# Turning the keys of the third block on with VectorE and GpSimd in place of TensorE, in a fused attention and feed-forward kernel

## Chip, cores and metric

The kernel runs on one core of one Trainium2 chip. The metric is the device time of one execution in microseconds (us); the time given is the median of three runs. The inputs and outputs are float32.

## What is computed

A gated linear recurrence over 768 steps gives the input of a two-layer feed-forward block with a squared ReLU:

```python
f = 1.0 / (1.0 + np.exp(-f_logit))
for t in range(S):
    state = f[:, :, t, :, None] * state + np.einsum('bhd,bhe->bhde', k[:, :, t], v[:, :, t])
    y[:, :, t] = np.einsum('bhd,bhde->bhe', q[:, :, t], state)
x = y.transpose(0, 2, 1, 3).reshape(B * S, H * D)     # 3072 x 384
h = x @ w_in                                          # 384 x 2048
r = np.maximum(h, 0.0)
out = (r * r) @ w_out                                 # 2048 x 384
```

with 4 batches, 8 heads, 768 steps and a head size of 48.

## The kernel before

The 768 steps are cut into six blocks of 128 steps (all four batches together, 512 columns). A **unit** is one block and one pair of heads: unit n has block n // 4 and pair n % 4. The first three units of a block are "own" units; the fourth has no rows of its own and works on rows that the other three have put aside in `last_kq` and `last_kn`. Units 0 to 7 (the first two blocks) run in a prologue whose order is written out by hand (FIRST, SECOND). What matters here starts after it.

From there the feed-forward runs as a row of **pieces** (`Moe.flow`): 16 pieces for the second block, 10 for the rest of the first, then 16 for each further block. A piece n is nine matmuls `up` (L244, tile `ph`), ScalarE's ReLU, square and cast (L254 to L256, tile `gh`), VectorE's remainder (L261, tile `gl`), and nine matmuls `down` of the piece two earlier (L271). Each product is made of three matmuls on halves of the float32 words. In the first 14 pieces VectorE and ScalarE also decode weights (L141 to L171).

Between pieces stand the **slots** of the attention: `SLOTS` says after which piece. The slot with unit n as the new one and n-1 as the old one issues on TensorE the updates of the state of unit n (L558, tile `shared`), its scores (L574) and the outputs of unit n-1 (L623, L632). The updates for the first 64 steps of each batch (c = 0) come first and those for the other 64 (c = 1) at the slot's end. All of them write one bank of PSUM. Between the two, GpSimd writes a flag (L768, `G.memset(tick, 0)`): it waits for the last c = 0 update, and the first c = 1 update waits for it.

What a unit needs before its slot is a list of stages, each with a piece relative to its slot (`STAGE_AT`, `BLOCKS_AT`):

- L and v: loads, on SyncE's queue
- G: the gate on ScalarE (L447)
- K: VectorE's scan of the keys (L452), GpSimd's two small clamps of 128x8 (L457, tiles `fkq` and `low`), VectorE's product (L458)
- Q: VectorE's reciprocal of the clamped column (L464), scan (L466) and product (L469)
- T: four TensorE transposes of the keys into PSUM (L514), for the units below `TURNED` = 13
- B: for the others, VectorE's transpose inside blocks of 32x32 (L528), then 16 copies of blocks on GpSimd (L533)
- N: for the units below 13 ScalarE's copy of the turned keys out of PSUM (L538, tile `kn`); for all of them ScalarE's copy of the put-aside columns (L540, `last_kn`)
- s: two copies of states on ScalarE (L487)

After a slot VectorE does the mask (L588) and the states (L603, L610) of the new unit, ScalarE and VectorE the cast and the remainder of the old unit's output (L652, L668).

Each engine works through its instructions in the order in which the compiled program has them. For VectorE, ScalarE, TensorE and SyncE this is the order of the code; GpSimd's comes from the same code, through the scheduler.

Of the kernel before, what the change touches and what calls it, by code (L numbers as in the profile page):

```python
# [13 lines left out]
F32 = mybir.dt.float32  # L14
F32R = mybir.dt.float32r
# [7 lines left out]
P = 128  # L23
B, H, S, D = 4, 8, 768, 48
DM, DFF = 384, 2048
HP = H // 2
C = 64
# [3 lines left out]
NT = B * TB  # L31
NZ = B * NC
# [9 lines left out]

LAG = 2
Q = 32
TURNED = 13
AHEAD = 4
LO = 6
SPLIT = 2
# [7 lines left out]

SLOTS = (13, 16, 19, 21, 23, 27, 31, 35, 39, 43, 47, 51, 55, 59, 63, 67, 71)
STAGE_AT = ((-6, 0, "Lv"), (-3, 1, "GK"), (-1, 0.5, "Q"), (-1, 1, "TN"), (1, 1, "s"))  # L60
BLOCKS_AT = ((-6, 0, "Lv"), (-3, 1, "GKB"), (-1, 0.5, "Q"), (0, 0.7, "N"), (1, 1, "s"))
LAST_AT = ((-6, 0, "v"), (1, 1, "s"))


# [295 lines left out]
    return t.rearrange("p (n t) -> p n t", t=C)  # L360


def scanned(t):
    return t.rearrange("p (n t) -> p n t", t=CZ)


def fast_path(ctx, psum, tc, moe, ident, low, flag, fkqT, vN, w, w4, out):
# [41 lines left out]
    class Unit:  # L409
# [93 lines left out]

        def turn(self):

            if self.blk < 2:
                self.pk = self.ps_a[0].tile([P, B, P], F32, tag="pk", name=f"pk{self.nm}")
            else:

                if not shared:  # L510
                    shared.append(self.ps_a[0].tile([P, B, P], F32, tag="pk", name="shared"))
                self.pk = shared[0]
            for b in range(B):
                nc.tensor.transpose(  # L514
                    out=self.pk[:, b], in_=self.kt[:, b * TB : (b + 1) * TB], identity=ident
                )

        def turn_blocks(self):


            if self.n < 14:
                both = self.wk([P, 2, NT], "ys")
                kb, kn = both[:, 0], both[:, 1]
            else:
                kb, kn = (
                    moe.gp.tile([P, NT], F32, tag=f"part{i}", name=f"turn{self.nm}_{i}", bufs=1) for i in range(2)
                )
            V.transpose(out=kb, in_=self.kt)  # L528
            kb, self.kn = (t.rearrange("p (b n) -> p b n", b=B) for t in (kb, kn))
            self.pk = self.kn  # L530
            for a in range(0, P, Q):
                for r in range(0, P, Q):
                    G.tensor_copy(out=self.kn[a : a + Q, :, r : r + Q], in_=kb[r : r + Q, :, a : a + Q])  # L533

        def turned(self):
            if self.n < TURNED:
                self.kn = self.wk([P, B, ROWS], "kn")
                nc.scalar.copy(out=self.kn, in_=self.pk[:, :, :ROWS])  # L538
            at = self.hp * (C - D)
            nc.scalar.copy(  # L540
                out=last_kn.rearrange("p b (h r) -> p b h r", h=2)[:, :, :, at : at + C - D],
                in_=self.pk.rearrange("p b (h r) -> p b h r", h=2)[:, :, :, D:],
            )
# [10 lines left out]

        def add_one(self, dd, b, c, h):

            rows, m = slice(c * C, (c + 1) * C), D if h or self.blk > 1 else C
            return nc.tensor.matmul(  # L558
                dd[h * C : h * C + m, c, b * D : (b + 1) * D],
                lhsT=self.kn[rows, b, h * C : h * C + m],  # L560
                rhs=self.vn[rows, b, h * D : (h + 1) * D], start=True, stop=True,
            )
# [81 lines left out]
        def upper(self):  # L644

            self.x = self.xs[self.blk]
            y = self.x[self.hp] if self.own else self.wk([ROWS, 2, NT], "ys", 1, F32R)
            if not self.own:
                self.x.append(y)
            self.y = [y[:ROWS, i].rearrange("p (b c t) -> p c b t", b=B, c=NC) for i in range(2)]  # L650
            self.py = self.py[:ROWS].rearrange("p c (b t) -> p c b t", t=C)
            nc.scalar.copy(out=self.y[0], in_=self.py)  # L652
# [26 lines left out]
        def stage(self, letters):  # L679
            for c in letters:  # L680
                {
                    "L": lambda: self.load(slice(0, 3)),
                    "f": lambda: self.load(slice(0, 1)),
                    "k": lambda: self.load(slice(1, 2), slice(2, 3)),
                    "v": lambda: self.load_v(),
                    "G": lambda: self.gates(),
                    "K": lambda: self.keys(),
                    "Q": lambda: self.queries(),
                    "m": lambda: self.move(),
                    "r": lambda: self.crossed(),  # L690
                    "T": lambda: self.turn(),
                    "B": lambda: self.turn_blocks(),
                    "N": lambda: self.turned(),
                    "D": lambda: self.add(),
                    "S": lambda: self.scores(),
                    "M": lambda: self.masked(),
                    "C": lambda: self.states(),
                    "s": lambda: self.crossed_states(),
                    "Y": lambda: self.outputs(),
                    "H": lambda: self.upper(),  # L700
                    "z": lambda: self.less(),
                    "X": lambda: self.lower(),
                    "g": lambda: self.parts((1,), G if self.blk < 2 else nc.sync),
                    "h": lambda: self.parts((0,), nc.sync),
                }[c]()
# [7 lines left out]
    )  # L713
    half = list(range(LO)), list(range(LO, NF))
    xs = {blk: moe.new_x(blk, blk) for blk in range(2)}
    units, decoding, shared = {}, {}, []

    for t in xs[0]:
        G.memset(t[C + 32 :].bitcast(F32), 0.0)
# [10 lines left out]
    def slot(old, new):  # L730

        ab = ps_a.tile([P, 2, 512], F32, tag="ab", name=f"ab{(new or old).nm}_{new is None}")
        rows = [[], []]
        if old:
            old.py = ab[:, :, : B * C]
            for c in range(NC):
                for b in range(B):  # L740
                    for part in range(2):
                        for h in (c, 1 - c):
                            rows[c].append((C, lambda a=(part, b, c, h): old.output_one(*a)))
        if new:
            new.sd = ab[:, :, B * C :]
            new.dd = shared[0].rearrange("p (c e) n -> p c (e n)", c=NC)[:, :, : B * D]
            adds = [
                [] if new.last_of(c) else [
                    (D, lambda a=(b, c, h): update(*a)) for b in range(B) for h in (c, 1 - c)
                ] for c in range(NC)  # L750
            ]
            for h in range(2):
                for b in range(B):
                    for c in (h, 1 - h):
                        rows[h].append((C, lambda a=(b, c, h): new.score_one(*a)))
            rows = [adds[0] + rows[0], rows[1] + adds[1]]
        seen = []

        def behind(ins, first):
            tc.add_manual_dep(ins, first.name, mybir.DependencyInfo(  # L760
                mybir.DependencyClass.Sync, mybir.DependencyReason.DATA
            ), reason="one bank")

        def update(b, c, h):
            ins = new.add_one(new.dd, b, c, h).ins
            if c == 0 and b == B - 1 and h:

                seen.append(G.memset(tick, 0).ins)  # L768
                behind(seen[0], ins)
            elif c and b == 0 and h:  # L770
                behind(ins, seen[0])

        at = [0, 0]
        while any(rows):
            r = min((r for r in range(2) if rows[r]), key=lambda r: at[r])
            cols, do = rows[r].pop(0)
            at[r] += cols
            do()
# [51 lines left out]
    with tc.manual_schedule(engines={ET.PE, ET.SP, ET.DVE, ET.Activation}):  # L830
# [13 lines left out]
        def hook(n, at, do):  # L844
            hooks.setdefault((max(n, 0), at), []).append(do)

        def third():
            early.close()
            moe.inputs(ctx)
            xs[2] = moe.new_x(2, 2)  # L850

# [2 lines left out]
        for n in range(1, NF - 1):  # L856
# [22 lines left out]
            hook(n, 0, before)  # L879
            hook(n, 0.5, after)  # L880
            hook(n, 0.7, last)
        hook(NF - 1, 0, third)
        late = [Unit(n, xs, (ps_a,)) for n in range(2 * HP, NBLK * HP)]
        for at, old, un in zip(SLOTS, (None, *late), (*late, None)):
            if un:
                for n, place, stage in LAST_AT if not un.own else STAGE_AT if un.n < TURNED else BLOCKS_AT:
                    hook(at + n, place, lambda un=un, stage=stage: un.stage(stage))
            hook(at, 1, lambda old=old, un=un: slot(old, un))
            if old:
                hook(at, 1, lambda old=old: old.stage("HX" if old.own else "HXhg"))  # L890
            if un:
                hook(at, 1, lambda un=un: un.stage("rMCm" if un.own else "rMC"))
# [238 lines left out]
```

## Time and profile before

| | |
|---|---|
| median of three runs | 485.92 us (485.27 to 486.57) |
| profiled execution, its own time | 483.37 us |
| span of the profiled execution | 481.7 us |
| TensorE matmuls busy | 468.2 us, 97% of the span |
| VectorE, ScalarE, GpSimd busy | 54%, 58%, 17% |
| granted TensorE clock, mean | 0.999 |

The profile is one execution, so durations are taken from it and a sum of them is set against its own time, 483.37 us. A group's row in the trace gives the busy time and the mean duration of one instruction, a row of the timeline its start and duration in us. The start-to-start distance of neighbours is what an instruction costs its engine; the recorded durations of matmuls overlap.

### The profile page before, as it was taken

To read this page: it belongs to the slowest core of one execution; us is meant where nothing else is said; L and a number is where in the kernel's file an instruction comes from. 1 tells how busy PE (TensorE), PEld (TensorE's weight loads), DVE (VectorE), ACT (ScalarE), POOL (GpSimd) and SP (SyncE) were. 2 spreads that over 40 slices of the span, in tenths; PEclk is the share of its full clock that TensorE was granted. 3 is DMA by queue.
4 is the path that set the end of the run, shared out by engine and by line. 5 is a ranking of instruction groups with operands and counts; after the bars stand their busy time and mean duration, and the time that the engine had idled before them with its cause. 6 is when DMAs were issued, how large, how long until landed. Compare 5 with 4: busy or idle time off the path is not lost. (4 is left out here: it accounts for less than half of the span.)

```text
span 481.7 us, 11552 instructions
## 1 busy us (share of the span) xinstructions
PE 468.2 (97%) x4763; PEld 384.9 (80%) x4763; DVE 261.5 (54%) x482; ACT 277.9 (58%) x562; POOL 80.0 (17%) x210
## 2 busy tenths in 40 slices
PE   5889999999999999999999999999999999999996
PEld 5767787888888888888888888888888888888884
DVE  7999976988966566643447443356353312221111
ACT  4778757787756555645546645545654543544441
POOL 6222010001010005150053150052350000000000
PEclk9999999999999999999999999999999999999999
DMA  8995235567114205332005332005300002100002
GB/s 292 282 310 141 66 95 182 191 221 254 28 31 141 86 2 125 95 97 80 1 2 127 95 95 83 1 1 122 98 12 3 2 0 34 67 0 2 1 0 71
DMA packets 22636, 42.60 MB, mean 88 GB/s; under 512 B 4512, under 2 KB 8128, under 8 KB 22576
## 3 DMA queue, kind: packets, MB, share of 16 engines
q1 hardware_dynamic: 22128, 40.86, 27.6%
q0 software_dynamic: 448, 0.92, 0.8%
q8 instruction: 39, 0.64, 0.6%
q14 instruction: 21, 0.17, 0.1%
HBM read 31.69 MB, written 4.72 MB: 76 GB/s over the span
## 5 line engine op out<-in xcount | busy, mean ns | idle before, releaser
L244 PE MATMUL ph<-x,w 128*128 128x512 f32 x864 | 215.1, 393 | 1.1 <-DVE gl L261 0.6
L244 PEld LDWEIGHTS ph<-x,w 128*128 128x128 f32 x864 | 160.0, 188 | 35.6 <-DVE gl L261 1.0
L271 PE MATMUL po<-gh,w 128*128 128x512 f32 x570 | 175.5, 389 | 0.0
L261 DVE TENSOR_TENSOR gl<-ph,gh 128x512 fp32r<-128x512 f32 x95 | 65.4, 688 | 160.0 <-ACT gh L256 159.7
L254 ACT ACTIVATE ph<-ph 128x512 f32<-128x512 f32 x96 | 55.9, 582 | 123.9 <-PE ph L244 123.7
L271 PEld LDWEIGHTS po<-gh,w 128*128 128x128 f32 x570 | 107.0, 188 | 22.3
L271 PE MATMUL po<-gl,w 128*128 128x512 f32 x285 | 111.1, 390 | 0.0
L271 PEld LDWEIGHTS po<-gl,w 128*128 128x128 f32 x285 | 53.5, 188 | 11.2
L255 ACT ACTIVATE ph<-ph 128x512 f32<-128x512 f32 x96 | 55.9, 582 | 3.0
L256 ACT CAST gh<-ph 128x512 fp32r<-128x512 f32 x95 | 55.8, 587 | 3.0
L533 POOL COPY turn<-turn 32x128 f32<-32x128 f32 x112 | 42.1, 376 | 8.3 <-DVE turn L528 3.7
L457 POOL TENSOR_SCALAR fkq<-fkq 128x8 f32<-128x8 f32 x18 | 12.9, 717 | 144.9 <-DVE fkq L452 128.2
L452 DVE TENSOR_TENSOR_SCAN fkq<-fz,dr 128x520 f32<-128x520 f32 x18 | 22.3, 1238 | 6.7 <-ACT fz L447 6.7
L169 ACT CAST w<-wa 128x384 fp32r<-128x384 f32 (+1 forms) x33 | 16.6, 513 | 14.8 <-DVE wa L156 11.7
L466 DVE TENSOR_TENSOR_SCAN fkq<-fz,dz 128x520 f32<-128x520 f32 x18 | 22.4, 1247 | 0.6
L623 PE MATMUL ab_False<-sc,vn 64*48 64x64 f32 (+1 forms) x480 | 20.7, 220 | 0.0
L141 ACT ACTIVATE wa<-raw 128x384 f32<-128x384 f32 (+1 forms) x33 | 18.1, 550 | 4.1 <-DMA raw<-in_w_dram 4.1
L668 DVE TENSOR_TENSOR x<-ab_False,x 112x512 fp32r<-112x512 f32 x12 | 8.3, 692 | 21.7 <-ACT x L652 21.7
L652 ACT CAST x<-ab_False 112x512 fp32r<-112x512 f32 x12 | 7.0, 587 | 22.5 <-PE shared L558 17.6
L632 PE MATMUL ab_False<-rx,sx 48*48 48x64 f32 (+1 forms) x240 | 19.4, 216 | 0.0
L768 POOL MEMSET flag<- 1x1 int32 x16 | 1.4, 88 | 106.2 <-PE shared L558 104.3
L152 DVE SCALAR_TENSOR_TENSOR wa<-raw,wa 128x384 int32<-128x384 int32 (+1 forms) x33 | 18.0, 552 | 0.7
(148 smaller groups left out, 495.3 us busy)
## 6 DMA issues: line engine op xcount, KB each, us to landing
raw<-in_w_dram SPq DMA_DIRECT2D x32, 384.0 KB, 4.2
fkq<-in_fkqT_dram SPq DMA_DIRECT2D x15, 768.0 KB, 6.0
vn<-in_vN_dram SPq DMA_DIRECT2D x24, 192.0 KB, 5.0
out_dram<-ob SPq DMA_DIRECT2D x14, 256.0 KB, 2.3
fkq<-in_fkqT_dram SPq DMA_DIRECT2D x9, 256.0 KB, 4.6
x<-ys SPq DMA_DIRECT2D x30, 64.0 KB, 2.3
last_kq<-fkq SPq DMA_DIRECT2D x28, 64.5 KB, 2.3
out_dram<-part SPq DMA_DIRECT2D x3, 256.0 KB, 2.4
```

The costliest lines, as they stand in the source:

```text
L141: nc.scalar.activation(a, upper_f, AF.Abs, scale=2.0**-112, **kw)
L244: self.nc.tensor.matmul(self.cur.ph[f], lhsT=w[:, i], rhs=x[:, j], start=first and n == 0, stop=last and n == 2)
L254: nc.scalar.activation(ph, ph, AF.Relu)
L255: nc.scalar.activation(ph, ph, AF.Square)
L256: nc.scalar.copy(out=gh, in_=ph)
L261: self.nc.vector.tensor_tensor(out=gl, in0=self.cur.ph.pop(f), in1=gh.bitcast(F32), op=ALU.subtract)
L271: self.nc.tensor.matmul(c.po[e], lhsT=l, rhs=r, start=f == c.fs[0] and i == 0, stop=f in c.ends and i == 2, skip_group_check=len(c.ends) > 1,)
L452: V.tensor_tensor_scan(out=rr[:, ::-1], data0=self.fz[:, NZ * CZ : 0 : -1], data1=dr[:, ::-1], initial=0.0, op0=ALU.mult, op1=ALU.add,)
L466: V.tensor_tensor_scan(out=pp, data0=self.fz[:, : NZ * CZ], data1=dz, initial=0.0, op0=ALU.mult, op1=ALU.add)
L533: G.tensor_copy(out=self.kn[a : a + Q, :, r : r + Q], in_=kb[r : r + Q, :, a : a + Q])
L623: nc.tensor.matmul(to[:m], lhsT=self.vn[rows, b, h * D : h * D + m], rhs=self.sc[rows, h, b], start=b == 0, stop=none and c == 0 and b == ...
L632: nc.tensor.matmul(to[:m], lhsT=s[rows, b * D : b * D + m], rhs=q[rows], start=False, stop=b == B - 1,)
```

## The change

The keys of units 8, 9, 10 and 12 (the own units from the third block on that were still turned by TensorE) are turned by VectorE's block transpose and GpSimd's 16 copies like those of the later units. The four transposes on TensorE and the copy `kn` of each fall away. The buffers are, for units 8 and 9, a tile of the prologue's pool, for unit 10 the tile `x2` of the third block's inputs, for unit 12 the tile `ys`. The stage B is split in b (VectorE) and B (GpSimd); three lists of stages set the pieces. The first two slots go from the 13th and 16th piece to the 15th and 17th. The pool of the prologue is closed after the second slot and not at the 15th piece, and the input tiles of the third block are made one by one when a unit's output is written. Unit 8's updates take 64 key columns for the first head of the pair, where it was 48. GpSimd's copies get an order-only dependence on the flag of the last slot.

```diff
-TURNED = 13
-SLOTS = (13, 16, 19, 21, 23, 27, 31, 35, 39, 43, 47, 51, 55, 59, 63, 67, 71)
-STAGE_AT = ((-6, 0, "Lv"), (-3, 1, "GK"), (-1, 0.5, "Q"), (-1, 1, "TN"), (1, 1, "s"))
-BLOCKS_AT = ((-6, 0, "Lv"), (-3, 1, "GKB"), (-1, 0.5, "Q"), (0, 0.7, "N"), (1, 1, "s"))
+SLOTS = (15, 17, 19, 21, 23, 27, 31, 35, 39, 43, 47, 51, 55, 59, 63, 67, 71)
+BLOCKS_AT = ((-6, 0, "Lv"), (-3, 1, "GKbB"), (-1, 0.5, "Q"), (0, 0.7, "N"), (1, 1, "s"))
+NEAR_AT = ((-6, 0, "Lv"), (-3, 1, "GK"), (-2, 1, "bB"), (-1, 0.5, "Q"), (0, 0.7, "N"), (1, 1, "s"))
+AHEAD_AT = (
+    (-6, 1, "Lv"), (-5, 1, "GKb"), (-4, 1, "B"), (-1, 0.5, "Q"), (0, 0.7, "N"), (1, 1, "s")
+)
...
-        def turn_blocks(self):
+        def blocks(self):
-            if self.n < 14:
-                both = self.wk([P, 2, NT], "ys")
-                kb, kn = both[:, 0], both[:, 1]
+            if self.n < 10:
+                if not turning:
+                    turning.append(pro.tile([P, 3, NZ * CZ], F32, tag="fkq", name="turning"))
+                kb, kn = (turning[0][:, i, :NT] for i in ((0, 1) if self.n == 8 else (2, 0)))
+            elif self.n < 14:
+                kb, kn = halved(
+                    self.wk([P, 2, NT], "ys") if self.blk > 2 else
+                    moe.xs[2].tile([P, 2, NT], F32, tag="x2", name=f"turn{self.nm}")
+                )
...
             V.transpose(out=kb, in_=self.kt)
...
+        def turn_blocks(self):
             for a in range(0, P, Q):
                 for r in range(0, P, Q):
-                    G.tensor_copy(out=self.kn[a : a + Q, :, r : r + Q], in_=kb[r : r + Q, :, a : a + Q])
+                    ins = G.tensor_copy(
+                        out=self.kn[a : a + Q, :, r : r + Q], in_=self.kb[r : r + Q, :, a : a + Q]
+                    ).ins
+                    for t in ticks[-1:]:
+                        tc.add_manual_dep(ins, t.name, mybir.DependencyInfo(
+                            mybir.DependencyClass.NoSync, mybir.DependencyReason.SCHED_ONLY
+                        ), reason="behind the last slot")
         def turned(self):
-            if self.n < TURNED:
+            if self.blk < 2:
                 self.kn = self.wk([P, B, ROWS], "kn")
                 nc.scalar.copy(out=self.kn, in_=self.pk[:, :, :ROWS])
...
-            rows, m = slice(c * C, (c + 1) * C), D if h or self.blk > 1 else C
+            rows, m = slice(c * C, (c + 1) * C), D if h or self.n > 2 * HP else C
...
+        def stages_of(un):
+            if not un.own:
+                return LAST_AT
+            return {9: NEAR_AT, 10: NEAR_AT, 12: AHEAD_AT}.get(un.n, BLOCKS_AT)
```

**GpSimd, units 8 to 10.** GpSimd's instructions from the clamps of unit 8 on, before (`fkq_0`, `fkq_1`, `fkq_2` with numbers 1502, 1632, 1763 are units 8, 9, 10; the last `fkq_0` is unit 12):

```order
L457 TENSOR_SCALAR fkq_0_1502<-fkq_0_1502 128x8
L457 TENSOR_SCALAR low<-fkq_0_1502 128x8
L768 MEMSET flag 1x1
L457 TENSOR_SCALAR fkq_1_1632<-fkq_1_1632 128x8
L457 TENSOR_SCALAR low<-fkq_1_1632 128x8
L768 MEMSET flag 1x1
L457 TENSOR_SCALAR fkq_2_1763<-fkq_2_1763 128x8
L457 TENSOR_SCALAR low<-fkq_2_1763 128x8
L768 MEMSET flag 1x1
L457 TENSOR_SCALAR fkq_0_2033<-fkq_0_2033 128x8
L457 TENSOR_SCALAR low<-fkq_0_2033 128x8
```

and in the change (1585, 1669, 1770 are units 8, 9, 10, and 2106 is unit 12; lines have moved by 7 to 23):

```order
L544 COPY turning<-turning 32x4x32 x16
L464 TENSOR_SCALAR fkq_1_1669<-fkq_1_1669 128x8
L791 MEMSET flag 1x1
L464 TENSOR_SCALAR low<-fkq_1_1669 128x8
L544 COPY turning<-turning 32x4x32 x16
L464 TENSOR_SCALAR fkq_2_1770<-fkq_2_1770 128x8
L791 MEMSET flag 1x1
L464 TENSOR_SCALAR low<-fkq_2_1770 128x8
L544 COPY turn_2_2088<-turn_2_2088 32x4x32 x16
L464 TENSOR_SCALAR fkq_0_2106<-fkq_0_2106 128x8
L791 MEMSET flag 1x1
L544 COPY ys_0_2148<-ys_0_2148 32x4x32 x12
```

Each flag now stands behind the 16 copies of its own slot's unit and behind the first clamp of the next unit.

**VectorE, from the last decoded weight to the work after the first slot.** Before (`sc_0`, `sp_73` and `state_79` are the mask and the states after the slot of unit 8; the rows SCALAR_TENSOR_TENSOR with 128x520 are the scans, in the trace TENSOR_TENSOR_SCAN):

```order
L171 TENSOR_TENSOR w_0_1783<-wa_0_1758,w_0_1783 128x384
L588 TENSOR_TENSOR sc_0_1832<-ab_0_False,mask 128x512
L603 TENSOR_TENSOR sp_73<-state_79,fkq_0_1502 112x192
L610 TENSOR_TENSOR state_79<-sp_73,shared 112x192
L603 TENSOR_TENSOR sp_73<-state_79,fkq_0_1502 112x192
L610 TENSOR_TENSOR state_79<-sp_73,shared 112x192
L452 SCALAR_TENSOR_TENSOR fkq_1_1632<-fz_72,dr 128x520
L458 TENSOR_TENSOR fkq_1_1632<-fkq_1_1632 128x512
L150 TENSOR_SCALAR wa_1_1845<-wa_1_1845 128x384
```

and in the change:

```order
L173 TENSOR_TENSOR w_1_1826<-wa_1_1802,w_1_1826 128x384
L459 SCALAR_TENSOR_TENSOR fkq_1_1669<-fz_72,dr 128x520
L465 TENSOR_TENSOR fkq_1_1669<-fkq_1_1669 128x512
L263 TENSOR_TENSOR gl_15_1856<-ph_15_1845,gh_15_1855 128x512
L605 TENSOR_TENSOR sc_0_1909<-ab_0_False,mask 128x512
L620 TENSOR_TENSOR sp_73<-state_79,fkq_0_1585 112x192
L627 TENSOR_TENSOR state_79<-sp_73,shared 112x192
L620 TENSOR_TENSOR sp_73<-state_79,fkq_0_1585 112x192
L627 TENSOR_TENSOR state_79<-sp_73,shared 112x192
L536 STREAM_TRANSPOSE turning<-fkq_1_1669 128x512
L471 RECIPROCAL dz<-fkq_1_1669 128x8
L473 SCALAR_TENSOR_TENSOR fkq_1_1669<-fz_72,dz 128x520
```

The block transpose of unit 9 now comes behind the mask and the states that wait for the end of unit 8's slot, and unit 9's scan stands behind the last decoded weight.

## Rows read from the trace of the kernel before

**Rows 1.** Waits of TensorE, longest first: us in total, times, longest

```profile
PE pk L514 <- DVE fkq L458: 2.0, 1, 2.0
```

**Rows 2.** Busy us (instructions) of PE, PEld, DVE, ACT, POOL, then clock and DMA

```profile
115.00:135.00 20.00, 19.98 (x149) 16.31 (x148) 19.34 (x36) 13.89 (x33) 3.10 (x5) 1.00 0.28 87
...
180.00:470.00 290.00, 290.00 (x2580) 239.91 (x2579) 116.20 (x194) 149.46 (x277) 56.59 (x155) 1.00 0.17 48
```

**Rows 3.** Timeline of TensorE, pieces 13 to 17: start, us, engine, line, operation

```profile
121.55 0.60 PE L514 MATMUL shared<-ident,fkq 128*128 128x128 f32 x4
...
124.05 0.39 PE L271 MATMUL po<-gl,w 128*128 128x512 f32 x1
...
126.18 0.24 PE L558 MATMUL shared<-vn,kn 64*48 64x48 f32 x1
...
127.00 0.25 PE L558 MATMUL shared<-vn,kn 64*48 64x48 f32 x2
...
127.50 2.34 PE L244 MATMUL ph<-x,w 128*128 128x512 f32 x9
...
131.72 2.20 PE L244 MATMUL ph<-x,w 128*128 128x512 f32 x9
133.76 0.39 PE L271 MATMUL po<-gl,w 128*128 128x512 f32 x1
...
140.47 0.24 PE L558 MATMUL shared<-vn,kn 64*48 64x48 f32 x1
...
141.89 0.20 PE L558 MATMUL shared<-vn,kn 64*48 64x48 f32 x1
...
142.39 0.96 PE L244 MATMUL ph<-x,w 128*128 128x512 f32 x3
```

**Rows 4.** Timeline of VectorE (one row of ScalarE), around the first two slots

```profile
123.18 0.59 ACT L256 CAST gh<-ph 128x512 fp32r<-128x512 f32 x1
...
125.41 0.69 DVE L261 TENSOR_TENSOR gl<-ph,gh 128x512 fp32r<-128x512 f32 x1
...
129.08 0.68 DVE L588 TENSOR_TENSOR sc<-ab_False,mask 128x512 f32<-128x512 f32 x1
...
131.18 1.23 DVE L452 TENSOR_TENSOR_SCAN fkq<-fz,dr 128x520 f32<-128x520 f32 x1
...
135.65 0.20 DVE L464 RECIPROCAL dz<-fkq 128x8 f32<-128x8 f32 x1
...
137.77 0.68 DVE L261 TENSOR_TENSOR gl<-ph,gh 128x512 fp32r<-128x512 f32 x1
...
145.88 1.23 DVE L452 TENSOR_TENSOR_SCAN fkq<-fz,dr 128x520 f32<-128x520 f32 x1
```

**Rows 5.** Timeline of GpSimd: a clamp, a flag and the 16 copies of unit 13

```profile
132.50 0.95 POOL L457 TENSOR_SCALAR fkq<-fkq 128x8 f32<-128x8 f32 x1 [5.55 <-DVE fkq L452]
...
141.13 0.09 POOL L768 MEMSET flag<- 1x1 int32 x1 [7.03 <-PE shared L558]
...
186.85 6.74 POOL L533 COPY ys<-ys 32x128 f32<-32x128 f32 x16 [0.47 <-DVE ys L528]
```

**Rows 6.** Unit 13's block transpose, then scan and product, and two copies beside them

```profile
186.01 0.71 DVE L528 STREAM_TRANSPOSE ys<-fkq 128x512 f32<-128x512 f32 x1
...
187.49 1.24 DVE L466 TENSOR_TENSOR_SCAN fkq<-fz,dz 128x520 f32<-128x520 f32 x1
188.76 0.69 DVE L469 TENSOR_TENSOR fkq<-fkq 128x512 f32<-128x512 f32 x1
...
187.50 1.31 POOL L533 COPY ys<-ys 32x128 f32<-32x128 f32 x1
...
188.85 0.75 POOL L533 COPY ys<-ys 32x128 f32<-32x128 f32 x1
...
L533 POOL COPY turn<-turn x112: 279/288/1267, 205.2 to 359.5; 32x128 f32<-32x128 f32 x112
```

**Rows 7.** The page, DMA issues: operation, count, size of each, median us to landing

```profile
fkq<-in_fkqT_dram SPq DMA_DIRECT2D x15, 768.0 KB, 6.0
```

More of the change, by code (lines that the diff above doesn't have):

```diff
@@ L360, in chunks, with halved @@
     return t.rearrange("p (n t) -> p n t", t=C)
+def halved(t):
+    t = t.rearrange("p a n -> p (a n)")
+    return t[:, :NT], t[:, NT:]
 def scanned(t):
@@ L504, in turn @@
         def turn(self):
[L506 to L512, printed above, removed]
+            self.pk = self.ps_a[0].tile([P, B, P], F32, tag="pk", name=f"pk{self.nm}")
             for b in range(B):
@@ L528, in turn_blocks @@
             V.transpose(out=kb, in_=self.kt)
-            kb, self.kn = (t.rearrange("p (b n) -> p b n", b=B) for t in (kb, kn))
+            self.kb, self.kn = (t.rearrange("p (b n) -> p b n", b=B) for t in (kb, kn))
             self.pk = self.kn
+        def turn_blocks(self):
             for a in range(0, P, Q):
                 for r in range(0, P, Q):
-                    G.tensor_copy(out=self.kn[a : a + Q, :, r : r + Q], in_=kb[r : r + Q, :, a : a + Q])
+                    ins = G.tensor_copy(
[5 more added lines that the diff above has]
+                        ), reason="behind the last slot")
         def turned(self):
-            if self.n < TURNED:
+            if self.blk < 2:
                 self.kn = self.wk([P, B, ROWS], "kn")
@@ L646, in upper @@
             self.x = self.xs[self.blk]
+            if self.blk == 2 and self.own:
+                self.x.append(moe.xs[2].tile([P, 2, NT], F32R, tag=f"x{self.hp}", name=f"x2_{self.hp}"))
             y = self.x[self.hp] if self.own else self.wk([ROWS, 2, NT], "ys", 1, F32R)
@@ L691, in stage @@
                     "T": lambda: self.turn(),
+                    "b": lambda: self.blocks(),
                     "B": lambda: self.turn_blocks(),
@@ L715, in fast_path @@
     xs = {blk: moe.new_x(blk, blk) for blk in range(2)}
-    units, decoding, shared = {}, {}, []
+    units, decoding, shared, ticks, turning = {}, {}, [], [], []
     for t in xs[0]:
@@ L744, in slot @@
         if new:
+            if not shared:
+                shared.append(ps_a.tile([P, B, P], F32, tag="pk", name="shared"))
             new.sd = ab[:, :, B * C :]
@@ L768, in update @@
                 seen.append(G.memset(tick, 0).ins)
+                ticks.append(seen[0])
                 behind(seen[0], ins)
@@ L849, in third @@
             moe.inputs(ctx)
-            xs[2] = moe.new_x(2, 2)
+            xs[2] = []
         halves = [(f, i) for f in half[1] for i in range(2)]
@@ L881, in fast_path @@
             hook(n, 0.7, last)
-        hook(NF - 1, 0, third)
         late = [Unit(n, xs, (ps_a,)) for n in range(2 * HP, NBLK * HP)]
+        def stages_of(un):
+            if not un.own:
+                return LAST_AT
+            return {9: NEAR_AT, 10: NEAR_AT, 12: AHEAD_AT}.get(un.n, BLOCKS_AT)
         for at, old, un in zip(SLOTS, (None, *late), (*late, None)):
             if un:
-                for n, place, stage in LAST_AT if not un.own else STAGE_AT if un.n < TURNED else BLOCKS_AT:
+                for n, place, stage in stages_of(un):
                     hook(at + n, place, lambda un=un, stage=stage: un.stage(stage))
             hook(at, 1, lambda old=old, un=un: slot(old, un))
+            if at == SLOTS[1]:
+                hook(at, 1, third)
             if old:
```

## Prediction

> **What bounds the kernel now.** I read the waits of TensorE first, then the stretches, then the timelines of the four engines between 115 and 200 us. The longest wait of TensorE in the whole execution is 2.0 us, in the prologue [rows 1]; between 180 and 470 us it is busy for 290.00 of 290.00 us [rows 2]. So whatever time leaves TensorE's own queue shortens the kernel, and whatever makes TensorE wait lengthens it by as much. The second thing to see is that VectorE is no free engine where the change puts work: from 115 to 135 us it is busy for 19.34 of 20.00 us, because the last weights are still being decoded [rows 2]. GpSimd is nearly idle there, with 3.10 us.
>
> **TensorE's saving.** A group of four transposes goes from 121.55 to the first `down` at 124.05, 2.50 us with the nine `up` behind it; nine `up` without transposes take 131.72 to 133.76, 2.04 us [rows 3]. That is 0.46 us for one unit and 4 x 0.46 = **1.84 us** for units 8, 9, 10 and 12, all of it on the path. The four copies `kn` on ScalarE were hidden beside TensorE's pieces and free nothing. This is the whole gain to be had.
>
> **What is put in its place** is, for each unit, a block transpose of 0.71 us on VectorE and 16 copies on GpSimd, and the wait of the slot for them. For unit 13, which went this way before, the copies start 0.84 us after the transpose and take 6.74 us together [rows 5, 6]. Most copies last 0.288 us, but the copy that meets VectorE's scan (1.24 us) lasts 1.31 us and the one that meets the product behind it (0.69 us) 0.75 us [rows 6]. The two lose 1.02 and 0.46 us, so 16 copies with nothing in their way are 6.74 - 1.48 = 5.26 us, 0.33 us each, and every pair of a scan and a product that VectorE runs beside them adds up to 1.48 us. The Trainium skill, page "SBUF", section "Who interferes with whom", says that a VectorE instruction with two SBUF inputs and a GpSimd instruction that reads SBUF shut each other out, the later one until the first has finished. The two long copies agree with it. By that rule the decoding of weights would hold the copies up as well, and the sum would lie towards the upper end that I give below.
>
> **Where the wait lands.** In the order of GpSimd the flag of a slot now stands behind the 16 copies of the slot's own unit and behind the first clamp of the next unit, and that clamp waits for VectorE's scan of the next unit's keys. TensorE needs the flag for the second half (c = 1) of the updates, and behind them in its queue stands the next piece. With one unit the second half starts 127.00 - 126.18 = 0.82 us into the slot, with two 141.89 - 140.47 = 1.42 us [rows 3]. The first half needs only the first eight copies. Three slots are at stake.
>
> *Slot 15 (unit 8).* Without transposes and without the slot at 13, piece 13 starts at 121.55; three pieces of 2 x 2.04 us, about 0.1 us of lead and 0.82 us bring TensorE to the second half at 134.7. The flag waits for unit 9's clamp, this for unit 9's scan, and this stands in VectorE's order behind the last decoded weight. Before, VectorE took from the `gl` at 125.41 to the reciprocal at 135.65, 10.24 us, to be through with that weight [rows 4]. In that stretch the change takes out the mask and states (129.08 to 131.18, 2.10 us), swaps unit 9's scan and product for unit 8's, and puts in the block transpose (0.71 us) and unit 8's reciprocal, scan and product (135.65 to 137.77, 2.12 us): 10.97 us. When that `gl` starts is not shown. VectorE is relieved of about 4.0 us ahead of it (unit 8's scan and product, and the same 2.12 us), which would be 121.4; ScalarE's cast, which it needs, ended at 123.77 before [rows 4]. I take 122.5, about the middle, since ScalarE's casts there are themselves late because of VectorE. Then the scan starts at 133.5 and ends at 134.7, the clamp (0.95 us, as in a row of this stretch), the flag (0.09 us) [rows 5] and the hand-overs end at 135.9. **Wait: 1.2 us**, bounds 0.1 and 2.5 us by the two ends of that `gl`. Unit 8's own copies, held up by decoding, end at about 135 and so hide behind the same wait.
>
> *Slot 17 (unit 9).* From the piece after slot 15, TensorE takes a piece of 127.50 to 131.72 = 4.22 us, one of 4.08, 0.1 of lead and 1.42: 9.8 us. The other way: mask and states 2.10 us (plus 0.1 until they start), 0.84 us to the first copy, the copies, a clamp (I take 0.8 us, as VectorE is quiet by then), flag and hand-overs 0.25: 4.1 us and the copies. Beside them VectorE runs a pair of scan and product twice, unit 9's queries and unit 10's keys: 5.26 + 2 x 1.48 = 8.2 us; with one pair 6.74. I take 7.8, since a copy that is under way when a scan starts isn't held up. **Wait: 4.1 + 7.8 - 9.8 = 2.1 us**, bounds 1.0 and 2.5.
>
> *Slot 19 (unit 10).* Here an old unit's output stands ahead: 142.39 to 145.88 = 3.49 us from the slot's end until VectorE's states are through [rows 3, 4]. The way is 3.49 + 0.84 + 7.8 + 1.05 = 13.2 us against 9.8. **Wait: 3.4 us**, bounds 2.3 and 3.8. From unit 12 on two pieces or more lie between, and its copies start behind the flag of slot 19, long before slot 23: nothing.
>
> **The rest at nothing, and why.** ScalarE's copies of `last_kn` now wait for GpSimd's last copy and stand ahead of the copies of the first sums out of PSUM; TensorE is waiting longer for the flag, which comes after that copy, and if that cover went, ScalarE would be what is late next. Unit 8's and 9's loads move behind weight loads in SyncE's queue, unit 12's behind three output stores, two moves and the second slot; a load lands 6.0 us after its issue [rows 7], for unit 12 at about 157 us, with its clamp needed only behind unit 10's copies, at about 161. If it came 4 us later still, it would set slot 19. The 64-column updates of unit 8 stream the same 48 columns; closing the pool later issues nothing.
>
> **Sum.** -1.84 + 1.2 + 2.1 + 3.4 = **+4.9 us**. The profiled execution took 483.37 us, so its like would take 488.3; it was 2.55 us under the median of the runs, and 485.92 + 4.9 = **490.8 us**. With all low bounds it is +1.6 (487.5), with all high ones +7.0 (492.9).
>
> **Rivals.** *Copies that are not held up.* If VectorE did not stand in GpSimd's way, the copies would take 5.26 us: slot 15 keeps its 1.2 us (a matter of VectorE's order alone), slot 17 loses nothing (9.4 against 9.8), slot 19 0.8: +0.2 us, 486.1. For it: only two of sixteen copies in that train were long. Against it: the same two rows.
>
> *The copies and clamps are in time* (the other side). The change then gives its 1.84 us, 484.1. It needs the flag to come 1.2 us sooner at slot 15, which an earlier `gl` alone can do, and the copies to come 2.1 and 3.4 us sooner at the next two slots, as they would if VectorE reached its block transposes without waiting for mask and states, or if the second half of the updates did not wait for that flag. It decides at slot 19: with a chain there under 9.8 us nothing is lost. Against it: 3.49 + 0.84 + 5.26 us without any hindrance is 9.6 already, ahead of clamp and flag.
>
> *The clock falls.* While TensorE works, its granted clock is 1.00 in both stretches [rows 2], the 2.4 GHz level. A wait of over 3 us is longer than any shown. If the clock fell to 1.2 GHz for one piece after slot 19, that piece would take 4.08 us more: 494.9. The Trainium skill, page "TensorE: Matmul & The Clock Gate", Part 1, says that the clock drops to half after the engine has been idle for a while. No row here shows it after a wait of this length.
>
> **How the numbers follow.** A measurement of this kernel can tell about 0.3% (1.5 us) from no change. I give the forecast 0.67, the clock 0.07, both slower by more than that; the unhindered copies 0.14, no change to be told; the copies in time 0.12, faster. So slower 0.74, same 0.14, faster 0.12. The range takes the forecast's bounds and, below, the second case: 486.0 to 493.0 us. It leaves out the gain and the fallen clock, some 0.19.
>
> **What would show it.** Right: TensorE has three new waits on GpSimd's flag of about 1.2, 2.1 and 3.4 us, in slots 15, 17 and 19 and in none later; the 16 copies of units 9 and 10 take over 7 us; the transposes of tile `shared` are gone and the four pieces behind them are 0.46 us shorter. Wrong: TensorE as busy as before in that stretch, a flag ahead of TensorE's second half, copies of unit 10 under 6 us, a new wait of ScalarE or on a load that sets the slot, or a granted clock under 1.00.

## The result and the profile after

The changed kernel takes **491.46 us** in the median of six runs (489.61 to 493.51), the kernel before beside it 485.78 us (484.58 to 486.57, six runs): a ratio of **1.0125**, 95% interval 1.0104 to 1.0147. The forecast was 490.8 us, slower. (The ratios here and below are formed over the runs, so they differ a little from the quotient of the two medians.) Lines have moved: `up` is L246, `down` L273, the updates L575, the clamps L464, GpSimd's copies L544, the flag L791.

The profiled execution is the slowest of the six (493.51 us, span 491.8 us). TensorE's waits in it from 115 us to 470 us, in the columns of [rows 1]:

```profile
PE shared L575 <- POOL flag L791: 4.2, 3, 1.7
PE shared L575 <- POOL turn L544: 1.4, 1, 1.4
```

Before, that stretch had none: these are the three slots, with slot 19 split into a wait for the first eight copies and one for the flag. The stretches, in the columns of [rows 2]:

```profile
140.00:146.00 6.00, 4.32 (x52) 3.54 (x45) 4.82 (x11) 2.15 (x5) 2.45 (x8) 1.00 0.09 15
152.00:158.00 6.00, 4.90 (x83) 4.07 (x75) 2.78 (x8) 3.85 (x9) 1.70 (x8) 1.00 0.48 156
164.00:170.00 6.00, 4.25 (x133) 3.71 (x134) 2.82 (x6) 1.69 (x4) 5.14 (x19) 1.00 0.43 139
180.00:470.00 290.00, 290.00 (x2699) 239.97 (x2698) 120.08 (x202) 150.12 (x280) 56.94 (x156) 1.00 0.17 48
```

TensorE loses 1.68, 1.10 and 1.75 us in three windows of 6 us (the third begins inside slot 19's first wait and misses 1.0 us of it) and nothing from 180 us on. The granted clock is 1.00 in all four. TensorE's timeline, in the columns of [rows 3], shows piece 13, the first and second half of the updates in the three slots, and the last nine `down`:

```profile
127.03 2.20 PE L246 MATMUL ph<-x,w 128*128 128x512 f32 x9
...
139.36 0.25 PE L575 MATMUL shared<-vn,turning 64*64 64x48 f32 x1
...
141.95 0.26 PE L575 MATMUL shared<-vn,turning 64*48 64x48 f32 x2 [1.68 <-POOL flag L791]
...
150.94 0.24 PE L575 MATMUL shared<-vn,turning 64*48 64x48 f32 x1
...
153.77 0.25 PE L575 MATMUL shared<-vn,turning 64*48 64x48 f32 x2 [1.10 <-POOL flag L791]
...
162.67 0.24 PE L575 MATMUL shared<-vn,turn 64*48 64x48 f32 x1
...
164.38 0.24 PE L575 MATMUL shared<-vn,turn 64*48 64x48 f32 x1 [1.39 <-POOL turn L544]
...
167.41 0.25 PE L575 MATMUL shared<-vn,turn 64*48 64x48 f32 x2 [1.37 <-POOL flag L791]
...
485.38 2.32 PE L273 MATMUL po<-held,w 128*128 128x512 f32 x9 [0.30 <-PEq L1095]
```

The last nine `down` of the kernel before:

```profile
475.25 2.33 PE L271 MATMUL po<-held,w 128*128 128x512 f32 x9 [0.30 <-PEq L1064]
```

I call a slot's wait what its second half starts late: its distance from the slot's first update, less the 0.82 us (one unit) or 1.42 us (two) of [rows 3]. That is 2.59 - 0.82 = **1.77 us** in slot 15, 2.83 - 1.42 = **1.41 us** in slot 17, 4.74 - 1.42 = **3.32 us** in slot 19. From the start of piece 13 to the start of the last `down` the change takes 485.38 - 127.03 = 358.35 us, before 475.25 - 121.55 = 353.70 us [rows 3]. The difference, **+4.65 us**, is the three waits less 1.84 us (+4.66). (Below, "from piece 13 on" always means this stretch, and its difference to 353.70. The expectations that say "to the end" count to the end of the last matmul, 2.3 us more on both sides.) The other 5.5 us by which this execution is longer lie ahead of piece 13, in the prologue, and the second profile below does not have them. Some 3.4 us of them arise near 40 us, where TensorE waits 1.85 us for ScalarE and has a granted clock of 0.50 for 3.4 us behind that wait.

GpSimd's timeline, in the columns of [rows 5]:

```profile
131.76 9.78 POOL L544 COPY turning<-turning 32x128 f32<-32x128 f32 x16 [0.40 <-DVE turning L536]
141.62 0.24 POOL L464 TENSOR_SCALAR fkq<-fkq 128x8 f32<-128x8 f32 x1
141.81 0.09 POOL L791 MEMSET flag<- 1x1 int32 x1
...
145.47 7.89 POOL L544 COPY turning<-turning 32x128 f32<-32x128 f32 x16 [3.29 <-DVE turning L536]
153.45 0.24 POOL L464 TENSOR_SCALAR fkq<-fkq 128x8 f32<-128x8 f32 x1
153.63 0.09 POOL L791 MEMSET flag<- 1x1 int32 x1
...
158.77 8.23 POOL L544 COPY turn<-turn 32x128 f32<-32x128 f32 x16 [4.76 <-DVE dz L471]
167.08 0.24 POOL L464 TENSOR_SCALAR fkq<-fkq 128x8 f32<-128x8 f32 x1
167.26 0.09 POOL L791 MEMSET flag<- 1x1 int32 x1
```

In all three slots the copies, the clamp and the flag follow each other without a gap, and TensorE starts 0.14 to 0.15 us after the flag's start. The trains of units 9 and 10 take 7.89 and 8.23 us (7.8 forecast); that of unit 8, beside the decoding, takes 9.78 us.

### The profile page after: what moved, and what is told of

The parts are those of the page before. It is cut to its first block, busy times and chain, and to the rows that moved or that the text cites. A ratio compares the mean times of both kernels' runs of the same rounds, so it can differ in the third digit from the quotient of the medians.

```text
span 491.8 us, 11596 instructions
## 1 busy us (share of the span) xinstructions
PE 469.1 (95%) x4747; PEld 385.9 (78%) x4747; DVE 264.8 (54%) x486; ACT 276.3 (56%) x558; POOL 106.3 (22%) x274
## 5 line engine op out<-in xcount | busy, mean ns | idle before, releaser
L246 PE MATMUL ph<-x,w 128*128 128x512 f32 x864 | 215.7, 394 | 0.6 <-DVE gl L263 0.6
L246 PEld LDWEIGHTS ph<-x,w 128*128 128x128 f32 x864 | 161.1, 189 | 35.6 <-DVE gl L263 1.0
L273 PE MATMUL po<-gh,w 128*128 128x512 f32 x570 | 175.5, 389 | 0.0
L273 PEld LDWEIGHTS po<-gh,w 128*128 128x128 f32 x570 | 107.0, 188 | 22.2
L273 PE MATMUL po<-gl,w 128*128 128x512 f32 x285 | 111.1, 390 | 0.0
L273 PEld LDWEIGHTS po<-gl,w 128*128 128x128 f32 x285 | 53.5, 188 | 11.2
L544 POOL COPY turn<-turn 32x128 f32<-32x128 f32 x128 | 49.8, 389 | 13.7 <-DVE dz L471 4.8
L464 POOL TENSOR_SCALAR fkq<-fkq 128x8 f32<-128x8 f32 x18 | 11.0, 610 | 135.5 <-DVE fkq L459 126.8
L791 POOL MEMSET flag<- 1x1 int32 x16 | 1.4, 89 | 84.8 <-PE shared L575 82.9
L640 PEld LDWEIGHTS ab_False<-sc,vn 64*48 64x48 f32 (+1 forms) x480 | 18.2, 126 | 0.0
```

Of the source, the lines that this page charges most:

```text
L246: self.nc.tensor.matmul(self.cur.ph[f], lhsT=w[:, i], rhs=x[:, j], start=first and n == 0, stop=last and n == 2)
L273: self.nc.tensor.matmul(c.po[e], lhsT=l, rhs=r, start=f == c.fs[0] and i == 0, stop=f in c.ends and i == 2, skip_group_check=len(c.ends) > 1,)
L544: ins = G.tensor_copy(out=self.kn[a : a + Q, :, r : r + Q], in_=self.kb[r : r + Q, :, a : a + Q]).ins
L640: nc.tensor.matmul(to[:m], lhsT=self.vn[rows, b, h * D : h * D + m], rhs=self.sc[rows, h, b], start=b == 0, stop=none and c == 0 and b == ...
```

## The experiments

**The changed kernel a second time**, for another profile.

> The changed kernel once more, for a second profile of it. From the start of piece 13 to the end the first profile takes 360.7 us against 356.0 us before, but it also reaches piece 13 5.5 us later, in a prologue whose TensorE order is the same. Theory (the prologue differs from one execution to the next, the slots do not): waits of 1.8, 1.4 and 3.3 us in slots 15, 17 and 19 again, each within 0.3 us; 360.5 to 361 us from piece 13 on; piece 13 starts anywhere between 121.5 and 127.5 us; the median stands 4.5 to 6 us over before. Rival (the change makes the prologue later too): piece 13 starts at 126 us or later again.

Median 490.44 us (489.17 to 491.42, six runs) against 484.88 us, ratio 1.0105 (1.0080 to 1.0130). TensorE's timeline in this execution:

```profile
121.96 2.20 PE L246 MATMUL ph<-x,w 128*128 128x512 f32 x9
...
134.30 0.25 PE L575 MATMUL shared<-vn,turning 64*64 64x48 f32 x1
...
136.89 0.26 PE L575 MATMUL shared<-vn,turning 64*48 64x48 f32 x2 [1.68 <-POOL flag L791]
...
137.49 3.47 PE L246 MATMUL ph<-x,w 128*128 128x512 f32 x9
...
157.77 0.24 PE L575 MATMUL shared<-vn,turn 64*48 64x48 f32 x1
...
162.34 0.32 PE L575 MATMUL shared<-vn,turn 64*48 64x48 f32 x2 [2.76 <-POOL flag L791]
...
481.81 2.32 PE L273 MATMUL po<-held,w 128*128 128x512 f32 x9 [0.30 <-PEq L1095]
```

and its stretches around the two waits:

```profile
138.40:141.80 3.40, 3.40 (x10) 2.63 (x9) 3.19 (x7) 0.77 (x2) 1.35 (x2) 0.50 0.01 2
...
162.30:165.70 3.40, 3.36 (x32) 2.76 (x33) 1.69 (x4) 1.39 (x3) 2.90 (x10) 0.50 0.52 198
```

Piece 13 starts at 121.96 us, so the changed kernel does not always come late out of its prologue, and the rival in that form is refuted. Of the other profiles only the one with the clamps moved (below) starts it late, at 125.76 us; the rest start it between 121.55 and 122.30 us. Whether the change makes a late prologue more frequent is not shown. The expectation for the slots missed, though. The waits are 1.77 us in slot 15, none in slot 17, 3.15 us in slot 19, and behind the first and the last of them the granted clock is 0.50 for 3.4 us, the 1.2 GHz level: the nine `up` at 137.49 take 3.47 us where 2.34 us is usual. From piece 13 on it is 359.85 us, +6.15. Waits less saving are 4.92 - 1.84 = 3.08 us; the other 3.07 us go to the two falls, some **1.5 us** each. The slower piece behind slot 15 also gave the copies of unit 9 the time they lacked: TensorE reaches the second half of slot 17 12.00 us behind that of slot 15, where in the first profile the flag let it go after 11.82 us. So slot 17 does not wait, and the two falls together make this profile only 1.50 us dearer than the first (6.15 against 4.65).

**The slots alone.**

```diff
-SLOTS = (13, 16, 19, 21, ...
+SLOTS = (15, 17, 19, 21, ...
```

> The kernel before with the first two slots at the pieces 15 and 17 and nothing else; the keys are still turned by TensorE. Theory (the loss is made by GpSimd's copies ahead of the flag): no train of copies stands ahead of a flag, so the waits at slots 17 and 19 are under 0.3 us each; at slot 15 the flag still stands behind unit 9's clamp, which alone would cost 0 to 1 us. Time 485.3 to 487 us, a ratio to before of 0.999 to 1.003. Rival (the two slots were moved to a stretch that has no room for them, whatever turns the keys): waits as in the change, about 2, 1.4 and 3.3 us, and 490 us or more.

484.45 us against 484.48 us, ratio 1.0003 (0.9984 to 1.0022): no difference that can be told (the ratio is as expected; the time lies below the expected range, as does the kernel before in this set of runs). Slots 15 and 17 don't wait. Slot 19 does, for 1.2 us, which neither side expected, and not for a flag but for ScalarE:

```profile
154.99 0.59 ACT L256 CAST gh<-ph 128x512 fp32r<-128x512 f32 x1 [4.49 <-DMA out_dram<-ob]
```

ScalarE's cast into a tile `gh` stands until an output store has left that buffer, and the copies `kn` and `last_kn` of unit 10 are queued behind it. From piece 13 on this execution takes 354.97 us, +1.27. So the new slots by themselves cost about 1 us at most by the times, through ScalarE, and no wait for GpSimd comes from them alone.

**Without the copies of units 8, 9 and 10.**

```diff
+            if self.n < 12:
+                self.kn = self.kb
...
+            if self.n < 12:
+                return
             for a in range(0, P, Q):
                 for r in range(0, P, Q):
                     ins = G.tensor_copy(
```

> The change, with the 48 copies of units 8, 9 and 10 on GpSimd left out: the updates read the keys as VectorE's block transpose leaves them, turned inside blocks only. Theory (the copies make the loss): the waits at slots 17 and 19 go to under 0.3 us, at slot 15 at most 1 us for unit 9's clamp is left; the TensorE time saved, 1.84 us, shows, and the time is 484 to 485 us, a ratio to before of 0.996 to 0.999. Rival (VectorE's late mask, states and block transposes, or the later loads, make the loss): the waits stay at 1 us or more at slots 17 and 19 and the time above 487 us.

484.04 us against 484.48 us, ratio 0.9985 (0.9966 to 1.0005). From piece 13 on 353.19 us, -0.51. All of TensorE's waits in the stretch, and what the clamps and flags of slots 15 and 19 do on GpSimd:

```profile
PE shared L579 <- POOL flag L795: 0.9, 2, 0.8
```

```profile
135.94 0.31 POOL L464 TENSOR_SCALAR fkq<-fkq 128x8 f32<-128x8 f32 x1 [9.29 <-DVE fkq L459]
136.19 0.09 POOL L795 MEMSET flag<- 1x1 int32 x1
...
156.44 0.68 POOL L464 TENSOR_SCALAR fkq<-fkq 128x8 f32<-128x8 f32 x1 [10.37 <-DVE fkq L459]
...
157.37 0.09 POOL L795 MEMSET flag<- 1x1 int32 x1
```

Of 6.5 us of waiting, 1.35 us are left (0.88 us in slot 15, none in slot 17, 0.47 us in slot 19, where at most 0.3 us was expected), and 1.35 - 1.84 = -0.49 is the -0.51 measured. So the copies make the loss. What is left is the clamp that waits for VectorE's scan: unit 9's in slot 15, as the prediction had it, and unit 12's in slot 19, which it had put at nothing.

**The clamps behind the flag.** Copies as in the change.

```diff
-NEAR_AT = (... (-2, 1, "bB"), ...
+NEAR_AT = (... (-2, 1, "pbB"), ...
-    (-6, 1, "Lv"), (-5, 1, "GKb"), (-4, 1, "B"), ...
+    (-6, 1, "Lv"), (-5, 1, "GKb"), (-4, 1, "pB"), ...
...
+            if self.n not in (9, 10, 12):
+                self.clamps()
...
+        def clamps(self):
...
+                ins = G.tensor_scalar(out=pe, in0=of, scalar1=LOWEST, scalar2=None, op0=ALU.max).ins
+                for t in ticks[-1:]:
+                    tc.add_manual_dep(ins, t.name, mybir.DependencyInfo(
+                        mybir.DependencyClass.NoSync, mybir.DependencyReason.SCHED_ONLY
+                    ), reason="behind the last slot")
```

> The change, with the clamps of units 9, 10 and 12 put behind the flag of the slot before, so that between the copies and the flag nothing is left on GpSimd. Theory (the copies themselves end last in all three slots, and the clamp adds its own 0.2 to 0.3 us behind them): each of the three waits gets 0.2 to 0.5 us shorter, 0.6 to 1.4 us in all, and TensorE still waits about 5 us in the three slots; a ratio to before of 1.006 to 1.011. Rival (the clamp that waits for unit 9's scan, behind the decoding, sets slot 15, as the prediction had it): the wait at slot 15 goes from 1.8 us to under 0.7 us while those of slots 17 and 19 stay, and the ratio is 1.008 to 1.012 too, so the waits decide, not the time.

490.90 us against 484.48 us, ratio 1.0108 (1.0073 to 1.0142). GpSimd around slot 15, and the TensorE row that waits for the flag:

```profile
130.50 9.77 POOL L552 COPY turning<-turning 32x128 f32<-32x128 f32 x16 [0.40 <-DVE turning L544]
140.32 0.09 POOL L800 MEMSET flag<- 1x1 int32 x1
...
140.47 0.26 PE L583 MATMUL shared<-vn,turning 64*48 64x48 f32 x2 [1.47 <-POOL flag L800]
```

The flag now follows the copies at once, and the waits are 1.56, 1.18 and 3.10 us, 0.66 us less in all. The rival is refuted: in slot 15 the copies end last, and the clamp behind them adds 0.2 us. From piece 13 on the granted clock is 0.50 once in this execution, for 3.4 us from 167.2 us, behind slot 19. The stretch takes 359.28 us (125.76 to 485.04), +5.58: waits less saving are 5.84 - 1.84 = 4.00 us, and the other 1.58 us go with this one fall. Ahead of it, near 40 us, this execution too has a wait for ScalarE (1.94 us) and 3.4 us at 0.50 behind it.

**Who holds GpSimd's copies up.** In the kernel before, six late units got two more VectorE instructions behind their block transpose.

```diff
+            spare = moe.gp.tile([P, NT], F32, tag="part2", name=f"spare{self.nm}", bufs=1)
+            for _ in range(2):
+                if self.n in (16, 17):
+                    V.tensor_tensor(out=spare, in0=kb, in1=self.kt, op=ALU.mult)
+                elif self.n in (18, 20):
+                    V.transpose(out=spare, in_=kb)
+                else:
+                    V.tensor_copy(out=spare, in_=kb)
```

> The kernel before, with two more VectorE instructions behind the block transpose of six late units; they write a tile that nobody reads. In units 16 and 17 they are products of two SBUF tiles, in 18 and 20 block transposes, in 21 and 22 plain copies. Before, the 16 copies of such a unit take 6.7 us, 5.26 us of them without hindrance. Theory (only a VectorE instruction with two SBUF inputs holds a GpSimd copy up): the train takes 7.5 to 7.8 us in units 16 and 17, with one or two more copies of about 0.75 us, and 6.7 us as before in the other four. Rival (any VectorE instruction beside it slows a copy, or none but the scan does): 7 us or more in all six, or 6.7 us in all six. The time stays within 0.5 us of before in either case, since late trains have 18 us and more.

One execution took 483.55 us. The trains of units 16, 18 and 21:

```profile
242.39 7.52 POOL L534 COPY turn<-turn 32x128 f32<-32x128 f32 x16 [0.54 <-DVE turn L528]
...
279.35 6.54 POOL L534 COPY turn<-turn 32x128 f32<-32x128 f32 x16 [0.56 <-DVE turn L528]
...
334.68 6.99 POOL L534 COPY turn<-turn 32x128 f32<-32x128 f32 x16 [0.54 <-DVE turn L528]
```

In the kernel before, these trains took 6.67 to 6.70 us. Two products make the train 0.8 us longer, two transposes do not, and two plain copies, each 0.43 us on VectorE, add 0.3 us, which the theory had not foreseen. (Units 17, 20 and 22 took 7.49, 6.54 and 6.99 us.) The Trainium skill, page "SBUF — State Buffer", section "Who interferes with whom", names two SBUF inputs and, under conditions, plain copies; the runs agree with both. The changed kernel shows it in its decoding, too:

```profile
133.04 0.69 DVE L263 TENSOR_TENSOR gl<-ph,gh 128x512 fp32r<-128x512 f32 x1
...
133.32 0.29 POOL L544 COPY turning<-turning 32x128 f32<-32x128 f32 x1
...
133.71 0.64 DVE L173 TENSOR_TENSOR w<-wa,w 128x384 fp32r<-128x384 f32 x1
...
133.98 0.52 POOL L544 COPY turning<-turning 32x128 f32<-32x128 f32 x1
```

The copy beside `gl`, one of whose inputs lies in PSUM, takes its usual 0.29 us; the one beside a weight's remainder, with both inputs in SBUF, takes 0.52 us.

**Unit 12 alone**, slots as before.

```diff
-TURNED = 13
+TURNED = 12
...
+AHEAD_AT = (
+    (-6, 1, "Lv"), (-5, 1, "GK"), (-4, 1, "B"), (-1, 0.5, "Q"), (0, 0.7, "N"), (1, 1, "s")
+)
```

> The kernel before with the change made for unit 12 alone: its four transposes leave TensorE, its block transpose and copies go to VectorE and GpSimd, loads and stages as in the change, slots as before. Theory (the waits come from the copies of units 8 to 10 alone): no wait for a flag over 0.3 us, 0.46 us less from piece 13 to the end (355.6 us against 356.0), and no difference that the times can tell. Rival (unit 12's clamps, now ahead of the flag of slot 19, wait for its later load): a wait of 1 to 4 us in slot 19 and 485 to 488 us.

487.07 us against 484.88 us, ratio **1.0044** (1.0024 to 1.0063): the rival, not the theory. Rows of ScalarE, GpSimd and TensorE, and a stretch behind the slot:

```profile
156.43 0.63 ACT L450 ACTIVATE fz<-fkq 128x512 f32<-128x512 f32 x1 [3.70 <-DMA fkq<-in_fkqT_dram]
...
158.48 0.68 POOL L460 TENSOR_SCALAR fkq<-fkq 128x8 f32<-128x8 f32 x1 [9.52 <-DVE fkq L455]
...
159.42 0.09 POOL L771 MEMSET flag<- 1x1 int32 x1
...
159.56 0.25 PE L561 MATMUL shared<-vn,kn 64*48 64x48 f32 x2 [1.77 <-POOL flag L771]
```

```profile
161.05:164.45 3.40, 3.40 (x9) 2.63 (x9) 2.98 (x7) 1.48 (x4) 0.11 (x1) 0.50 0.31 116
```

Unit 12's load comes behind three output stores. Gate, scan and both clamps follow it, and slot 19's flag stands behind the clamps: a wait of 2.1 us, and a fall of the clock behind it. From piece 13 (here 122.25) to the last `down` (479.12) it is 356.87 us, +3.17: 2.09 - 0.46 and some 1.5 us of clock. In the change, unit 10's copies cover this wait.

**The copies split between GpSimd and ScalarE**, with the clamps behind the flag.

```diff
-            for a in range(0, P, Q):
+            for a in range(0, C if self.n < 11 else P, Q):
                 for r in range(0, P, Q):
                     ins = G.tensor_copy(
...
+        def turn_rest(self):
+            for a in range(C, P, Q):
+                for r in range(0, P, Q):
+                    nc.scalar.copy(
+                        out=self.kn[a : a + Q, :, r : r + Q], in_=self.kb[r : r + Q, :, a : a + Q]
+                    )
```

> The change, with the clamps behind the flags as in the run with the clamps alone, and of the 16 copies of units 8, 9 and 10 only the eight for the first 64 steps on GpSimd; ScalarE makes the other eight, late in the piece ahead of the slot. Theory (the train of 16 copies of about 8 us on one engine makes the loss, half of it leaves room): GpSimd is through 4 us sooner, waits under 0.5 us in each slot, and the 1.84 us of TensorE show: 484 to 485.5 us, a ratio to before of 0.996 to 0.999. Rival (the start of the copies, behind the states and the block transpose, is late already, or ScalarE's eight copies and then its ReLU and squares come late): waits of 1 us and more stay at slot 19, or a new wait of TensorE on ScalarE's tiles, and 486 to 489 us.

484.12 us against 484.48 us, ratio 1.0003 (0.9983 to 1.0022). From piece 13 on 352.29 us, -1.41: the waits are nearly gone, as the theory had it, and 484.12 us lies in its range, but the ratio does not: beside this kernel before the times show no gain. With two more of unit 10's copies on ScalarE:

```diff
-                for r in range(0, P, Q):
+                for r in range(0, C if self.n == 10 and a else P, Q):
                     ins = G.tensor_copy(
...
-            for a in range(C, P, Q):
-                for r in range(0, P, Q):
+            for a in range(Q if self.n == 10 else C, P, Q):
+                for r in range(C if a < C else 0, P, Q):
                     nc.scalar.copy(
```

> The split version once more, with ten of unit 10's 16 copies on ScalarE and six on GpSimd. The split version took 354.6 us from piece 13 to the end, 1.4 us less than before, with 0.2 us and 0.4 us of waiting left in slots 15 and 19. Theory: the wait at slot 19 goes to about 0, 354.0 to 354.4 us from piece 13 on, and a ratio to before of 0.995 to 0.9985. Rival (ScalarE is late with the gate or the ReLU of the piece behind): a wait of TensorE for ScalarE of 0.3 us or more, and nothing gained over the first split.

484.40 us against 484.88 us, ratio 0.9988 (0.9972 to 1.0004), just above the expected range. The stretch of the slots, and GpSimd's train of unit 8, now of eight copies:

```profile
115.00:180.00 65.00, 65.00 (x819) 53.69 (x818) 49.30 (x88) 48.80 (x115) 19.22 (x51) 1.00 0.29 91
```

```profile
126.63 3.69 POOL L555 COPY turning<-turning 32x128 f32<-32x128 f32 x8 [0.40 <-DVE turning L547]
```

TensorE is busy for 65.00 of 65.00 us, and from piece 13 on it takes 351.92 us (121.90 to 473.82), -1.78: the forecast saving of 1.84 us is there once nothing waits. In the same set of runs the change took 490.44 us, 1.2% more. That the split beats the kernel before is not shown: its profiled execution took 483.21 us against 483.37 us. Of its gain, 0.35 us were lost ahead of piece 13, and about 1.1 us behind the last matmul, where its span goes on for 5.2 us against 4.1 us (5.0 us in the first split). Why is open.

## Why the prediction was right, and where it was off

**TensorE's saving, 1.84 us:** right, 1.78 us in the last run.

**Slot 17, 2.1 us forecast, 1.41 us in the first profile.** The copies were right (7.8 us, measured 7.89), held up by two pairs of scan and product. The clamp was put at 0.8 us; behind the copies, with VectorE quiet, it takes 0.24 us. That is nearly all of the difference.

**Slot 19, 3.4 us forecast, 3.32 us measured.** The parts were each a little off and cancel: from slot 17's end to the first copy 158.77 - 154.27 = 4.50 us (4.33 forecast), copies 8.23 us (7.8), then clamp, flag and hand-overs 0.4 us (1.05). That the total came so close is in part luck.

**Slot 15, 1.2 us forecast, 1.77 us in both profiles.** Here the named cause was only second. VectorE's way was forecast well: unit 9's scan starts 139.00 - 127.03 = 11.97 us behind the start of piece 13, where the forecast had 11.95. The step that failed is "unit 8's own copies, held up by decoding, end at about 135 and so hide behind the same wait". The prediction shows no sum for that 135. The copies take 9.78 us. Ten of the sixteen are longer than 0.5 us, each beside a VectorE instruction with two SBUF inputs: six beside the decoding, 1.7 us longer in all than the usual 0.29 us each, and four beside two pairs of scan and product (unit 8's queries, unit 9's keys), 2.8 us longer. So they end 1.1 us later than forecast, measured from piece 13's start (141.54 - 127.03 = 14.5 us, where the forecast had 13.4). Without copies the clamp alone gave 0.88 us of wait; with the clamp out of the way the copies alone gave 1.56 us. Over the three slots, 0.57 us too little here and 0.69 us too much in slot 17 cancel, so the agreement of the sum (6.50 us of waits, 6.7 forecast) is better than that of its terms; that is luck.

**The rest at nothing.** `last_kn` and the loads cost nothing that shows in the change. That unit 12's load and clamps hide behind unit 10's copies was right, but the cover is thin: with the copies gone 0.47 us show, with unit 12 moved alone 2.1 us.

**The rivals.** *Copies that are not held up* is refuted by the trains of 7.89 and 8.23 us. *Copies and clamps in time* needed what the splits provide: half of each train on another engine. *The clock falls* was given 0.07 as a case apart, with 4.08 us for a whole piece behind slot 19. What the runs show in its place is a cost of about 1.5 us for each fall, in some executions, behind slot 15 as well: no fall from piece 13 on in the first profile, two in the second, where the first of them takes the place of slot 17's wait. With none the change costs 4.65 us from piece 13 on, with two 6.15 us; the difference of the medians, 5.68 us in the first set of runs and 5.56 us in the second, lies between, though it also holds whatever the prologues differ by. The forecast's 4.9 us was right through its waits in the first profile; that it is some 0.7 us under the medians fits the falls of the clock, which no run isolates.

## What to carry to other kernels

Where one engine is the bound, work moved off it saves only what its new engine delivers in time: 0.46 us of TensorE per unit was exchanged for trains of 7.9 to 9.8 us ahead of a flag that TensorE needs. Read the order of the receiving engine up to the next instruction that the bound engine waits for, and size each train with what runs beside it, counting every neighbouring instruction that holds it up. A wait hidden behind a longer one comes out when the longer one is mended, as unit 12's load shows.

## What the runs showed of the hardware

TensorE's clock can fall behind a wait much shorter than the prediction had in mind. Idle times of 1.68 and 2.76 us (second profile) and 1.77 us (unit 12 alone) were each followed, at their end or about 1.5 us behind it, by 3.4 us at 0.50; so were the 1.59 us in slot 19 of the run with the clamps moved (1.7 us behind its end), and the 1.85 and 1.94 us in two prologues. The same 1.68 us in slot 15 of the first profile was not. The Trainium skill, page "TensorE: Matmul & The Clock Gate", Part 1, says that the clock drops to half after the engine has been idle; these rows agree, but the first profile's slots show that it need not. In the six profiles whose slots wait for less than 1.3 us it did not fall after piece 13 until the last matmul.

ScalarE's copies of the same 32x128 blocks are not held up by VectorE. Rows of the three engines in the first split, for unit 9:

```profile
140.04 1.32 DVE L484 TENSOR_TENSOR_SCAN fkq<-fz,dz 128x520 f32<-128x520 f32 x1
...
140.31 1.14 POOL L555 COPY turning<-turning 32x128 f32<-32x128 f32 x1
...
140.72 2.44 ACT L566 COPY turning<-turning 32x128 f32<-32x128 f32 x8
```

Beside the scan one copy on GpSimd takes 1.14 us; eight on ScalarE, beside the same scan and the product behind it, take 2.44 us, 0.31 us each. The eight for units 8 and 10 take 2.48 and 2.45 us.
